# The first batch's v in whole loads: four small loads taken out of a load order

## The chip, the cores and the metric

One core of a Trainium2 chip runs the whole program. The metric is the device time of one execution in microseconds (us). Other engines than TensorE, which does the matrix products (PE in the profile), are VectorE (DVE), ScalarE (ACT), GpSimd (POOL) and SyncE (SP). Loads from memory are issued by an engine's instruction stream and carried out by sixteen DMA engines.

## The reference, cut to what matters

```python
# q, k, v: (8 batches, 8 heads, 576 positions, 64)
scores = scale * np.matmul(q, k.transpose(0, 1, 3, 2))
mask = np.abs(pos[:, None] - pos[None, :]) <= 32
scores = np.where(mask, scores, -1000000000.0)
attn = softmax(scores)
attn_out = np.matmul(attn, v)
x = attn_out.transpose(0, 2, 1, 3).reshape(4608, 512)
h = x @ w_in                     # 512 x 2048
g = np.where(h >= 1, h, np.where(h <= -1, 0.0, (h + 1) ** 2 / 4))
out = g @ w_out                  # 2048 x 512
```

Attention in a sliding window of 32 positions to either side, then a two-layer network with a smoothed ReLU between the layers. The inputs are float32 in memory; the kernel computes in bfloat16, and the loads that GpSimd issues convert on the way.

## The kernel before, in words

**Tiling.** The token axis of the second part (4608) is cut into 18 tiles of 256 tokens (TB). For each tile, eight steps `a` (NF = 8) project 256 of the 2048 hidden columns each: line 489, eight matmuls of 128x256, two pieces of w_in to a step. From step 72 to 135 the steps are wide (line 514). ScalarE and VectorE turn the projected sums `hp` into `gT` (lines 533 to 540). The second product, with w_out, follows eight steps behind; up to step 39 partly in half-width pairs (line 464, `pair`), later in units (line 449). One variable `a` counts all steps, 160 in all, and the list `ev` holds what else is done after a step.

**Attention.** The softmax part of the eight batches is cut into pieces, put between these steps by a hand-written table (`at`, `sl`). `scores` multiplies k and q, `sums` multiplies the exponentials with v and with ones, and `xT` takes the quotients. v lies in `vn` as 18 chunks of 64 positions a pair of heads: chunks 0 to 8 for one head row, 9 to 17 for the other. `sums` over the first 256 positions read chunks 0 to 4 and 9 to 13; the remaining chunks are first read in steps 3 to 5.

**The start.** The first batch comes in halves: `load_half` brings positions 0 to 287 of q and k, then 288 to 575. While they are under way TensorE multiplies zeros (`keep_warm`). Then come the transposes, scores, sums and quotients of the first 256 positions, and step 0 begins. The second halves of q and k are transposed after step 1 (`tposes`, 189), the second batch's q after step 10 and its k after step 12 (lines 415 and 416).

**Loads.** All loads but the first half of q go through GpSimd's queue, in the order of the program text. Before the change this order is:

- k of batch 0, first half, two loads (L86)
- v of batch 0, chunks 0 to 13, four loads (L107, called in lines 132 and 136)
- w_in's first four pieces (L111); a piece is 256 columns for 64 partitions, 128 KB on the chip
- q and k, second half, four loads (L86)
- four times: a piece of w_in, then chunks 14 to 17 of one of v's four parts (lines 149 and 150)
- six more pieces of w_in, the first quarter of half of w_out (L116), w_in's last two, three more of w_out
- q and k of batch 1 (L93), v of batch 1 in four whole loads (L107), the other half of w_out, then batch 2

Batches 3 to 7 are loaded at set steps later.

**Waits.** The framework puts the semaphores in. A matmul waits for the loads that write the region that it reads; a load on GpSimd's queue can also wait, for an older load to land.

Of the kernel before, what the change touches and what calls it, by code (L numbers as in the profile page):

```python
# [14 lines left out]
def kernel(  # L15
# [19 lines left out]
    nc = tc.nc  # L35
# [3 lines left out]
    NC = S // 64  # L39
# [38 lines left out]
    qn, kn, vn = {}, {}, {}  # L78
# [20 lines left out]
            nc.gpsimd.dma_start(out=x[:, :, h], in_=src[b, NY * h:NY * h + NY].rearrange("y s d -> (y s) d")  # L99
                                .rearrange("(u p) d -> p u d", p=128))  # L100

    def load_v(b, n, c0=0, c1=2 * NC):
        if b not in vn:
            vn[b] = nat.tile([128, 2 * NC, 2, D], BF, name="vn", tag="vn", bufs=3)
        h, a = divmod(n, 2)
        y = NY * h + 2 * a
        nc.gpsimd.dma_start(out=vn[b][64 * a:64 * a + 64, c0:c1, h], in_=v[b, y:y + 2].rearrange("y s d -> (y s) d")  # L107
                            .rearrange("(c r) d -> r c d", r=64)[:, c0:c1])

    def load_w_in(c0, c1, h):  # L110
        nc.gpsimd.dma_start(out=w_in[64 * h:64 * h + 64, :, c0:c1],  # L111
# [11 lines left out]
    for h in range(2):  # L123
# [5 lines left out]

    step = early.tile([128, 257], BF, name="step")  # L130
    V.memset(step, 0.0)
    load_v(0, 0, 0, 14)
    P.affine_select(out=step, in_=step, compare_op=ALU.is_ge, fill=-1.0, base=-65, channel_multiplier=-1,
                    pattern=[[1, 257]])
    for n in range(1, 4):
        load_v(0, n, 0, 14)
    V.memset(ones, 1.0)
    for t in qTs:
        V.memset(t[:, 0:PAD], 0.0)
# [4 lines left out]
    def put(todo):  # L144
        for fn, *x in todo:
            fn(*x)

    w = [(load_w_in, c, c + 256, h) for c in range(0, DFF, 256) for h in range(2)]
    put(w[:4] + [(load_half, 1, t, h) for t in range(2) for h in range(2)]
        + [x for n in range(4) for x in (w[4 + n], (load_v, 0, n, 14, 2 * NC))] + w[8:14])  # L150
    put([(load_w_out, 0, 0, 4)] + w[14:])
    put([(load_w_out, 0, k, k + 4) for k in range(4, 16, 4)] + [(load_rows, 1, t) for t in range(2)])
    put([(load_v, 1, n) for n in range(4)])
# [264 lines left out]
    for b in range(LONG + 1, B):  # L418
        a = sl[5 * (b - 1) - 7] - 17
# [75 lines left out]
    for a in range(NF * NB + 2 * NF):  # L495
# [11 lines left out]
        if a < NF * NB:  # L507
            if wide:
                n, f = divmod(a - WIDE[0], 2 * NF)
                t = WIDE[0] // NF + 2 * n  # L510
# [6 lines left out]
            else:  # L517
                t, f = divmod(a, NF)
# [30 lines left out]
        if a >= 40:  # L549
            n = (4, 3, 3)[a % 3] if a < 88 else 4  # L550
# [36 lines left out]
```

## Time and profile before

| | us |
|---|---|
| median of 3 runs | 310.57 (310.31 to 310.81) |
| the profiled execution | 310.31 |
| its span in the profile | 308.5 |
| PE busy | 293.6 (95% of the span) |
| VectorE busy | 240.0 (78%) |
| ScalarE busy | 191.6 (62%) |
| GpSimd busy | 80.4 (26%) |
| mean granted clock of TensorE | 0.998 |

The profile is of one execution. Its span runs from the first to the last instruction; the device time is somewhat longer. "Busy" of PE counts matmuls whose ends are modelled, so 95% doesn't mean PE at its peak. GpSimd's figure counts the time that it takes to issue loads. A wait is given with what ended it; in the chain of waits each row has its start, its length and what it was.

### The profile page before, as it was taken

The page shows a single profiled execution, that of the slowest core. Times are in us where ns is not written, and L with a number is a line of the kernel's source. Part 1 is how long each engine was busy: PE and PEld are TensorE (multiplying, and loading weights), DVE is VectorE, ACT ScalarE, POOL GpSimd, SP SyncE. Part 2 cuts the span into 40 slices and gives each one's busy share as a digit, 9 for nine tenths or more (in the row PEclk, how much of TensorE's full clock was granted, in tenths as well). Part 3 has the DMA queues.
Part 4 walks back from the last instruction along what each step waited for, and adds up shares of the span by engine and source line. Part 5 has one row for each costly group of instructions (what it writes and reads, how often), then busy time and mean ns, then how long its engine had stood idle before and what let it go on. Part 6 is the DMA issues. An engine that isn't in the chain of part 4 may idle for free.

```text
span 308.5 us, 7943 instructions
## 1 busy us (share of the span) xinstructions
PE 293.6 (95%) x3350; PEld 181.4 (59%) x3388; DVE 240.0 (78%) x376; ACT 191.6 (62%) x320; POOL 80.4 (26%) x98
## 2 busy tenths in 40 slices
PE   8877999999999999999999999999999999999995
PEld 4555878876666666666654544444445444446644
DVE  3277468888988989998999998888888888878700
ACT  3786786838766758686766666765666654444311
POOL 8897762009106405402800910000000000000000
PEclk9999999999999999999999999999999999999999
DMA  9999999999999999998999993550001000000121
GB/s 150 188 142 184 197 189 162 170 181 101 150 182 119 172 202 111 169 151 130 144 124 187 121 165 51 113 114 34 36 34 37 34 36 35 36 34 34 54 84 68
DMA packets 137779, 35.67 MB, mean 116 GB/s; under 512 B 122256, under 2 KB 133520, under 8 KB 137744
## 3 DMA queue, kind: packets, MB, share of 16 engines
q0 software_dynamic: 103584, 18.06, 81.1%
q1 hardware_dynamic: 34016, 16.81, 25.5%
q8 instruction: 26, 0.43, 0.6%
q10 hardware_dynamic: 144, 0.29, 0.4%
q14 instruction: 9, 0.07, 0.1%
HBM read 36.70 MB, written 9.44 MB: 150 GB/s over the span
## 4 chain that ended last, share of the span: by engine, by line
PE 85%; DMA 7%; POOL 4%; issue 2%; ACT 1%; POOLq 0%; ACTq 0%
PE op L449 34%; PE hp L489 20%; PE hp L514 18%; PE bb L295 6%; PE op L464 4%; DMA qn<-in_q_dram 3%; PE bb L229 2%; POOL w_in L111 2%; DMA w_in<-in_moe_w_in_dram 2%; DMA qh<-in_q_dram 2%; POOL vn L107 1%; PE op L440 1%; PE tp L189 1%; ACT pt L237 1%; POOL kh L86 0%
## 5 line engine op out<-in xcount | busy, mean ns | idle before, releaser
L533 ACT ACTIVATE rr<-hp 128x512 f32<-128x512 f32 x144 | 85.6, 595 | 88.1 <-PE hp L489 43.7
L449 PE MATMUL op<-w_out,gT 128*128 128x512 bf16 x460 | 119.5, 379 | 5.0 <-issue 4.8
L539 DVE TENSOR_TENSOR mx<-hp,rr 128x512 f32<-128x512 f32 x137 | 94.4, 689 | 25.6 <-ACT rr L533 23.7
L540 DVE SCALAR_TENSOR_TENSOR gT<-rr,mx 128x512 bf16<-128x512 f32 x137 | 94.8, 692 | 4.7
L489 PE MATMUL hp<-xT,w_in 128*128 128x256 bf16 x640 | 83.1, 273 | 3.3 <-DMA w_in<-in_moe_w_in_dram 2.9
L489 PEld LDWEIGHTS <-w_in 128*128 128x128 bf16 x640 | 61.8, 98 | 23.9 <-DMA w_in<-in_moe_w_in_dram 2.8
L449 PEld LDWEIGHTS <-gT 128*128 128x128 bf16 x496 | 46.1, 98 | 45.2
L514 PE MATMUL hp<-xT,w_in 128*128 128x512 bf16 x256 | 65.7, 379 | 0.0
L514 PEld LDWEIGHTS <-w_in 128*128 128x128 bf16 x256 | 25.1, 98 | 30.2
L99 POOL DMA_DIRECT2D qn<-in_q_dram x12 | 14.6, 1221 | 89.7 <-DMA kT<-kn 67.3
L237 ACT ACTIVATE pt<-bb 128x1024 bf16<-128x1024 f32 (+1 forms) x33 | 32.7, 1002 | 4.7 <-PE bb L229 3.1
L107 POOL DMA_DIRECT2D vn<-in_v_dram x36 | 29.7, 851 | 5.0 <-DMA w_out<-in_moe_w_out_dram 4.2
L307 DVE TENSOR_TENSOR xT<-bb,rc 128x512 bf16<-128x512 f32 (+1 forms) x32 | 21.0, 657 | 9.3 <-ACT rc L302 8.4
L453 ACT COPY osb<-op 128x512 f32<-128x512 f32 x31 | 18.0, 580 | 11.4 <-PE op L449 11.1
L302 ACT ACTIVATE rc<-lr 128x512 f32<-128x512 f32 (+2 forms) x40 | 23.5, 587 | 1.3
L301 ACT ACTIVATE lr<-bb 128x512 f32<-128x512 f32 (+2 forms) x40 | 22.0, 551 | 0.1
L203 DVE TENSOR_TENSOR pt<-pt,mask 128x1024 bf16<-128x1024 bf16 (+1 forms) x33 | 20.3, 614 | 0.5 <-ACT pt L237 0.5
L295 PE MATMUL bb<-pt,ones 64*64 64x256 bf16 (+3 forms) x352 | 19.6, 255 | 0.3
L295 PE MATMUL bb<-pt,vn 64*64 64x128 bf16 (+3 forms) x712 | 18.2, 204 | 0.0
L464 PE MATMUL op<-w_out,gT 128*128 128x256 bf16 x128 | 16.5, 273 | 1.0 <-DMA w_out<-in_moe_w_out_dram 1.0
L295 PEld LDWEIGHTS <-ones 64*64 64x64 bf16 x352 | 10.3, 105 | 11.9 <-issue 11.9
L295 PEld LDWEIGHTS <-vn 64*64 64x64 bf16 x712 | 16.7, 107 | 0.0
(61 smaller groups left out, 141.6 us busy)
## 6 DMA issues: line engine op xcount, KB each, us to landing
out_dram<-osb SPq DMA_DIRECT2D x35, 256.0 KB, 2.3
vn<-in_v_dram POOLq DMA_DIRECT2D x28, 144.0 KB, 11.1
qn<-in_q_dram POOLq DMA_DIRECT2D x12, 288.0 KB, 6.3
kn<-in_k_dram POOLq DMA_DIRECT2D x12, 288.0 KB, 8.5
w_in<-in_moe_w_in_dram POOLq DMA_DIRECT2D x16, 128.0 KB, 4.9
w_out<-in_moe_w_out_dram POOLq DMA_DIRECT2D x4, 256.0 KB, 7.9
w_out<-in_moe_w_out_dram POOLq DMA_DIRECT2D x2, 512.0 KB, 14.3
kh<-in_k_dram POOLq DMA_DIRECT2D x4, 144.0 KB, 5.2
```

Of the source, the lines that this page charges most:

```text
L107: nc.gpsimd.dma_start(out=vn[b][64 * a:64 * a + 64, c0:c1, h], in_=v[b, y:y + 2].rearrange("y s d -> (y s) d") .rearrange("(c r) d -> r c ...
L237: A.activation(p, ps[:, :, :w * n].rearrange(like, y=m), AF.Exp, scale=D ** -0.5)
L295: nc.tensor.matmul(bb[HD[h], a, o + c0:o + c1], ones[HD[a]] if c is None else vn[b][HD[a], c, h], p(a, h), start=n == 0, stop=True, skip_g ...
L301: A.activation(lr[:, :, :D0], bb[:, :, D0:2 * D0], AF.Ln)
L302: A.activation(rc[:, :, :D0], lr[:, :, :D0], AF.Exp, scale=-1.0)
L449: nc.tensor.matmul(op[tt], gT[:, j, home(tt // 2), 128 * (tt % 2):128 * (tt % 2) + 128], w_out[:, j], start=j == 0, stop=j == 15)
L464: nc.tensor.matmul(o[:, tt], gT[:, j, p, 128 * tt:128 * tt + 128], w_out[:, j, 256 * half:256 * half + 256], start=not done, stop=len(done ...
L489: nc.tensor.matmul(hp[:, j], w_in[:, kk, 256 * f + 128 * j:256 * f + 128 * j + 128], xT[:, kk, r0:r0 + TB], start=first and n == 0, stop=l ...
L514: nc.tensor.matmul(hp.rearrange("p n t -> p (n t)"), w_in[:, kk, 128 * f:128 * f + 128], xT[:, kk, r0:r0 + 2 * TB], start=n == 0, stop=n == 3)
L533: A.activation(rr, hp, AF.Relu, scale=0.5, bias=0.5)
L539: V.tensor_max(mx, hp, rr)
L540: V.scalar_tensor_tensor(g, rr, 1.0, mx, op0=ALU.min, op1=ALU.mult)
```

## The change

The four small loads of batch 0's chunks 14 to 17 go, and the four early loads bring all 18 chunks. `load_v` loses its range of chunks.

```diff
-    def load_v(b, n, c0=0, c1=2 * NC):
+    def load_v(b, n):
...
-        nc.gpsimd.dma_start(out=vn[b][64 * a:64 * a + 64, c0:c1, h], in_=v[b, y:y + 2].rearrange("y s d -> (y s) d")
-                            .rearrange("(c r) d -> r c d", r=64)[:, c0:c1])
+        nc.gpsimd.dma_start(out=vn[b][64 * a:64 * a + 64, :, h], in_=v[b, y:y + 2].rearrange("y s d -> (y s) d")
+                            .rearrange("(c r) d -> r c d", r=64))
...
-    load_v(0, 0, 0, 14)
+    load_v(0, 0)
...
-        load_v(0, n, 0, 14)
+        load_v(0, n)
...
-    put(w[:4] + [(load_half, 1, t, h) for t in range(2) for h in range(2)]
-        + [x for n in range(4) for x in (w[4 + n], (load_v, 0, n, 14, 2 * NC))] + w[8:14])
+    put(w[:4] + [(load_half, 1, t, h) for t in range(2) for h in range(2)] + w[4:14])
```

Its name: "Second batch's q transposed in slot 10 instead of 11; w_in in pieces of 256 columns throughout, in place of: Second q transposed in slot 10; w_in in 256-column pieces; last 4 of 18 chunks of the first".

## The prediction

> **What bounds the kernel now.** I read the chain of waits first, then the sums of TensorE's (PE's) waits, then the table by two-microsecond windows. The end is PE's: the page gives PE 85% of the chain that ended last and DMA 7%. So I ask where PE still waits for something else, and PE's sums of waits answer: for pieces of w_in and w_out, 3.9 us, plus 4.8 us of "issue", spread in 30 gaps of at most 0.2 us that nothing here touches.
>
> ```profile
> PE op L449 <- issue: 4.8, 30, 0.2
> PE hp L489 <- DMA w_in<-in_moe_w_in_dram: 2.9, 4, 0.9
> PE op L464 <- DMA w_out<-in_moe_w_out_dram: 1.0, 2, 0.7
> ```
>
> In order of time these waits are at 17.62 (0.92 us), 22.42 (0.89), 26.07 (0.69), 27.35 (0.25), 28.79 (0.41) and 30.55 (0.73). After 36.07, where the second batch's q is transposed, PE has no wait for a load left. What the loads cost is therefore settled by the time at which PE gets past 36.07, and the chain shows who set that (start, duration, what):
>
> ```profile
> 6.12 2.38 POOL w_in L111 x4
> 8.49 5.62 DMA qh<-in_q_dram
> 14.12 0.28 issue
> 14.40 0.61 POOL w_in L111
> 15.01 0.61 POOL vn L107
> 15.62 0.61 POOL w_in L111
> ...
> 16.25 0.62 POOL vn L107
> ...
> 16.90 2.41 POOL w_in L111 x4
> 19.32 5.94 DMA w_in<-in_moe_w_in_dram
> 25.25 0.28 issue
> 25.54 10.49 DMA qn<-in_q_dram
> ...
> 36.07 1.20 PE tp L189 x36
> ```
>
> The reader is to see three things. First, GpSimd (POOL) issues loads, and what ends its pauses is the landing of an older load, 0.28 us earlier. Counting its loads in order, the 19th (14.40) waits for the 11th, the 35th (25.54) for the 27th, and the 43rd (36.31, q of batch 2) for the 35th. I conclude that eight loads may be under way and each new one waits for the eighth before it. Second, from 14.40 to 19.32 POOL issues without a pause: the chain is POOL's time. Third, two of the small v pieces, at 15.01 and 16.25, stand in that chain.
>
> The windows (start and end, length, then busy time and count of PE, PE weight loads, DVE, ACT, POOL, clock, DMA, GB/s) show what that costs the transfers:
>
> ```profile
> 18.00:20.00 2.00, 2.00 (x44) 1.37 (x42) 1.59 (x3) 1.22 (x3) 2.00 (x5) 1.00 1.25 120
> 20.00:22.00 2.00, 1.53 (x54) 1.06 (x51) 1.27 (x3) 2.00 (x5) 1.95 (x3) 1.00 1.27 154
> 22.00:24.00 2.00, 1.58 (x37) 1.26 (x38) 1.42 (x3) 1.85 (x4) 1.66 (x3) 1.00 1.03 129
> 26.00:28.00 2.00, 1.68 (x14) 1.39 (x15) 1.97 (x5) 1.24 (x3) 1.43 (x3) 1.00 1.47 202
> ```
>
> From 26 to 36 the five windows move 202, 190, 199, 210 and 206 GB/s, mean 201. The five from 16 to 26 move 154, 120, 154, 129 and 172, mean 146. A pair of a 128 KB w piece and a 32 KB v piece takes POOL 1.23 us, which supplies 164 KB (in thousands of bytes) / 1.23 = 133 GB/s. The dip looks like short supply.
>
> **What goes.** Four load_v calls of 4 chunks leave POOL, from 11.52, 12.96, 15.00 and 16.25. Each cost 0.61 to 0.66 us of POOL, one of the eight places for 3.4 to 5.3 us, and 32 KB of transfer.
>
> **What is added.** The same 32 KB joins each of the first four v loads. Two prices.
> POOL: batch 1's whole v loads take 1.71 us for two, 0.855 each; today's first takes 0.83 and the next three 2.29, 0.763 each. So 0.02 + 3 x 0.092 = 0.30 us, and w_in's first piece goes out at 6.42, not 6.12.
> Transfer: these are rows of 128 bytes on the chip, and the stretch from 6 to 8 us, almost all v, moved
>
> ```profile
> DMA packets 2375, 0.31 MB, mean 154 GB/s; under 512 B 2367, under 2 KB 2375, under 8 KB 2375
> ```
>
> so a piece costs 32.8 KB / 154 = 0.21 us, four 0.85 us. All that is issued behind v lands later by 0.30 (if only POOL counted) to 0.85 (if the DMA engines are never idle there). The engines' slices all read 9 from 6 to 14 us, so I take 0.7.
>
> **Who is hit early.** v's fourth load lands at 10.0 (5.30 plus 4.7) and would land near 10.7; its first use is 10.55, so the first softmax chain is late by 0.15 to 0.35 us. w_in's first four pieces land by 12.65, then 13.35; the projection that needs the last of them is at 13.5 or later. The second half's k lands at 15.95, then 16.65, used at 15.91: its copies have 0.6 us of slack behind VectorE's queue (L537 at 17.02). The first PE wait that grows is 17.62, for w_in's sixth piece. It is 0.7 later less the 0.21 of the one small v piece ahead of it: 0.5 us. PE is then 0.5 late.
>
> **What is won.** In the new order the loads 15 to 24 are w_in pieces without a gap, and the 19th is now w_in's ninth. It waits for the 11th (q, 14.12 + 0.7) plus 0.28: issued at 15.10 against 16.90 today. Three more follow at 0.60 each (2.41 / 4), none held by its eighth predecessor (k's last lands at 16.65, plus 0.28 = 16.93, and that load is due at 16.9). The thirteenth piece waits for the fifth, 16.60 + 0.7 + 0.28 = 17.6, against 19.32. That is 1.7 us earlier. Its landing took 5.94 us. Seven 128 KB pieces are then ahead or in flight where today one 32 KB, one w_in and four more stand, some 0.2 MB more; against that the queue no longer runs dry. I add 0.2. So it lands at 23.75 against 25.25, and q of batch 1, released by it and then 10.49 us under way, lands 1.5 us earlier, at 34.5.
>
> Bounds for this step: at most the whole dip is filled, (201 - 146) GB/s x 10 us = 550 KB, at 201 GB/s 2.7 us. At least 0, if the engines are slow in that stretch for a reason of their own, because the bytes ahead of q are the same in both orders. Of these, 1.5 is nearest to the chain's own rows.
>
> **Can PE use it?** From 17.62 to 36.07 PE waited 0.89 + 0.69 + 0.25 + 0.41 + 0.73 = 2.97 us after the first wait, so 0.5 late at the start leaves 2.5 to gain: enough. ScalarE is nearly full from 18.71 to 26.67 and starts 0.5 late; it makes up about 0.25 in its gaps there and had 0.47 us idle ahead of 27.14. No PE step up to 36.07 hangs on it longer than that. Behind 36.07, k lands at 39.3 (26.27 plus 13.0) for a use at 39.99, v of batch 1 at 44.1 for 45.2, w_out's second half at 46.8 for 48.1. These stand behind the same queue, so they move with q, and their slack of 0.7 to 1.3 us stays. The later loads are placed by PE's own steps. Sum: 310.31 (profiled execution, span 308.5 and 1.8 around it) - 1.5 = 308.8; the median before is 0.26 above that execution, so **309.1**.
>
> **A rule that speaks against it.** In 18 to 24 us VectorE is busy 1.27 to 1.59 us of 2 while the transfers sag. The Trainium skill (SBUF — State Buffer, section on the two separate sides) says that GpSimd cannot write descriptors for its loads while some VectorE operations hold the port that they share. By that the sag follows VectorE's work, stays after the change, and the sum is 310.6 with nothing won. The trace speaks only half for it: from 26 to 28 VectorE is busy 1.97 us and 202 GB/s are moved, though from a longer queue.
>
> **Rivals.** *The sag is not POOL's supply.* For it: from 20 to 24, with no small piece left to issue, POOL issues 128 KB per 0.61 us (215 GB/s) and yet only 154 and 129 are moved. Against it: w_in's first four pieces, issued alike, went at 168 to 195. Then q lands when it does now, the first 0.5 us is paid at 17.62 and taken back at 26.07 and 28.79: 310.5, between 310.2 and 310.9.
> *The v loads cost far more than 0.21 each.* Batch 1's four whole loads, issued at 27.59, 28.44, 29.77 and 30.81, land 13.0 to 13.3 us later, 1.0 to 1.3 us apart; today's four 14-chunk loads land between 8.2 and 10.0, 0.6 apart. At 1.0 apart all behind v is 1.6 late and the w_in chain still wins 0.9. To decide for slower, the delay at 14.12 must pass the 2.5 us between 14.40 and 16.90, by which w_in's ninth piece goes out sooner. At 1.3 apart, 4 x 0.7 = 2.8, and with POOL's 0.30 ahead of it 3.1, that piece is issued 0.6 later than now, q lands 0.6 later: 311.2. Against it: batch 1's loads shared the engines with w_out, and the stretch from 6 to 8 us shows such rows at 154 GB/s.
> *The name tells of more than the edit does.* Second q in slot 10 (L416) and 256-column pieces (L148) stand in the kernel already; only v's split goes. That adds no time of its own.
>
> **Chances.** Forecast 0.58, no supply effect 0.26, v far dearer 0.16. Alone, the forecast's range is 308.2 to 310.0. For 8 in 10 it must take in the second case and part of the third: **308.1 to 311.0**. 0.2% of 310.57, 0.62 us, is about what a measurement can tell from no change. Faster by more: 0.57; within: 0.27; slower: 0.16.
>
> **What would show it.** Right: the chain from 14 us on has w_in issues only, w_in's ninth at about 15.1; the windows from 18 to 24 move over 170 GB/s; PE's waits for w_in sum to under 2 us though the first grows to about 1.4; q of batch 1 is transposed near 34.6. Wrong: w_in's thirteenth piece lands at 25 again, or the first wait exceeds 3 us, or a new wait appears at k, v or w_out of the second batch.

## The result, and the profile after

| | before | changed |
|---|---|---|
| median of 6 runs each, us | 310.66 (310.31 to 311.26) | 308.20 (307.61 to 309.32) |
| ratio | | 0.9926, 95% interval 0.9904 to 0.9948 |
| profiled execution, us | 310.31 | 309.32 |
| its span, us | 308.5 | 307.6 |

The change is worth 2.46 us, by the interval 1.6 to 3.0. The profiled execution of the changed kernel is the longest of its six and that of the kernel before the shortest, so the profiles show only 1.0 us of that. Lines of the changed kernel stand one lower than before (L488 is the projection, L463 the pair).

PE's waits for w_in and w_out (us in all, times, longest) fell from 3.9 to 2.3 us. A wait of 0.3 us at 7.37, for the first half of k, is new:

```profile
PE hp L488 <- DMA w_in<-in_moe_w_in_dram: 2.1, 3, 1.1
PE op L463 <- DMA w_out<-in_moe_w_out_dram: 0.2, 1, 0.2
PE tp L188 <- DMA kh<-in_k_dram: 0.3, 1, 0.3
```

The chain of waits (start, duration, what) up to the transposition of the second batch's q:

```profile
6.64 1.80 POOL w_in L111 x3
8.44 6.91 DMA w_in<-in_moe_w_in_dram
15.34 0.28 issue
15.63 3.01 POOL w_in L111 x5
18.64 6.54 DMA w_in<-in_moe_w_in_dram
25.18 0.28 issue
25.46 9.56 DMA qn<-in_q_dram
...
35.07 1.20 PE tp L188 x36
```

The v issues are gone from the chain, and 36.07 has become 35.07. But a new link stands in front: w_in's fourth piece, issued at 8.44, landed 6.91 us later, where before the four took 4.5 to 4.8. GpSimd (POOL) needed its place among the eight and issued w_in's eighth piece only at 15.63.

The windows (length, busy time and count of PE, PE weight loads, VectorE, ScalarE, POOL; clock, DMA, GB/s last) show the sag filled: 171, 169 and 185 GB/s where 120, 154 and 129 stood.

```profile
18.00:20.00 2.00, 1.34 (x23) 0.99 (x18) 2.00 (x4) 1.58 (x3) 1.91 (x5) 1.00 1.40 171
20.00:22.00 2.00, 1.98 (x46) 1.28 (x44) 1.60 (x3) 1.64 (x3) 2.00 (x4) 1.00 1.36 169
22.00:24.00 2.00, 2.00 (x61) 1.56 (x64) 1.23 (x3) 2.00 (x5) 2.00 (x3) 1.00 1.35 185
```

### The profile page after: what moved, and what is told of

Read it like the earlier page. It is cut to its first block, busy times and chain, and to the rows that moved or that the text cites. A ratio compares the mean times of both kernels' runs of the same rounds, so it can differ in the third digit from the quotient of the medians.

```text
span 307.6 us, 7939 instructions
## 1 busy us (share of the span) xinstructions
PE 292.6 (95%) x3350; PEld 180.9 (59%) x3388; DVE 239.9 (78%) x376; ACT 191.3 (62%) x320; POOL 78.4 (25%) x94
## 4 chain that ended last, share of the span: by engine, by line
PE 85%; DMA 7%; POOL 3%; issue 2%; ACT 1%; POOLq 0%; ACTq 0%
PE op L448 34%; PE hp L488 20%; PE hp L513 18%; PE bb L294 6%; DMA w_in<-in_moe_w_in_dram 4%; PE op L463 4%; DMA qn<-in_q_dram 3%; PE bb L228 2%; POOL w_in L111 2%; POOL vn L107 1%; PE op L439 1%; PE tp L188 1%; ACT pt L236 1%; POOL kh L86 0%; PE bb L253 0%
## 5 line engine op out<-in xcount | busy, mean ns | idle before, releaser
L488 PE MATMUL hp<-xT,w_in 128*128 128x256 bf16 x640 | 83.1, 273 | 2.6 <-DMA w_in<-in_moe_w_in_dram 2.1
L488 PEld LDWEIGHTS <-w_in 128*128 128x128 bf16 x640 | 61.7, 98 | 23.0 <-issue 3.1
L107 POOL DMA_DIRECT2D vn<-in_v_dram x32 | 27.8, 901 | 4.3 <-DMA w_out<-in_moe_w_out_dram 3.8
L463 PE MATMUL op<-w_out,gT 128*128 128x256 bf16 x128 | 16.5, 273 | 0.2 <-DMA w_out<-in_moe_w_out_dram 0.2
```

The costliest lines, as they stand in the source:

```text
L107: nc.gpsimd.dma_start(out=vn[b][64 * a:64 * a + 64, :, h], in_=v[b, y:y + 2].rearrange("y s d -> (y s) d") .rearrange("(c r) d -> r c d", ...
L463: nc.tensor.matmul(o[:, tt], gT[:, j, p, 128 * tt:128 * tt + 128], w_out[:, j, 256 * half:256 * half + 256], start=not done, stop=len(done ...
L488: nc.tensor.matmul(hp[:, j], w_in[:, kk, 256 * f + 128 * j:256 * f + 128 * j + 128], xT[:, kk, r0:r0 + TB], start=first and n == 0, stop=l ...
```

## The experiments

Every kernel ran beside the kernel before on the same chip, and ratios are to that. A small load is one of the four of 32 KB. All 13 profiles taken after the prediction, and the one before, agree in one thing: from the start of the q transposition to the end of the execution it is 274.2 to 274.3 us (310.31 - 36.07, 309.32 - 35.07, and so on). So in the profiles the time differs only by what a kernel does up to that point, and the point is given with each.

| kernel | median, us | ratio (95% interval) | q transposed in its profile |
|---|---|---|---|
| changed, again | 308.11 | 0.9926 (0.9911 to 0.9942) | 34.59 |
| + POOL's time | 308.86 | 0.9941 (0.9922 to 0.9960) | 33.49 |
| + tiny loads | 311.10 | 1.0024 (1.0014 to 1.0035) | 36.48 |
| + five holds | 311.93 | 1.0046 (1.0029 to 1.0063) | 38.20 |
| + one hold | 311.00 | 1.0022 (1.0007 to 1.0037) | 36.56 |
| before, no late v | 307.52 | 0.9903 (0.9885 to 0.9921) | 33.32 |
| before, late v in a block | 309.85 | 0.9982 (0.9967 to 0.9996) | 35.87 |
| before, 512-column pieces | 311.47 | 1.0020 (0.9999 to 1.0042) | 37.54 |
| changed, 512-column pieces | 307.98 | 0.9919 (0.9896 to 0.9943) | 33.41 |
| block and 512-column pieces | 308.48 | 0.9940 (0.9920 to 0.9960) | 36.11 |
| changed, last two of 512 | 308.51 | 0.9932 (0.9917 to 0.9946) | 35.15 |

### What of a small load costs: POOL's time, its place, or its packets

A small load takes POOL some 0.62 us, one of eight places, and 32 KB of transfer. Three kernels bring one or two of these, or the waits alone, back into the changed kernel. The first, POOL's time alone:

```diff
+    idle = const.tile([128, 512], FP, name="idle")
+    def spend():
+        P.memset(idle, 0.0)
...
-    put(w[:4] + [...] + w[4:14])
+    put(w[:4] + [...] + [x for n in range(4) for x in (w[4 + n], (spend,))] + w[8:14])
```

> The changed kernel, with four fillings of a spare tile on POOL (about 0.6 us each) at the points where the four small v loads were: POOL's time comes back, but no place among the eight, no packets. If POOL's time is what was won: about 1.7 us of the gain goes, 309.9 to 310.5. If it was the places or the transfers: as the changed kernel, 308.2 within 0.5.

The second, POOL's time and the place, with 8 KB each:

```diff
+    def load_spare(n):
+        h, a = divmod(n, 2)
+        nc.gpsimd.dma_start(out=spare[64 * a:64 * a + 64, 0, h], in_=v[0, NY * h + 2 * a, 0:64])
...
+    put(w[:4] + [...] + [x for n in range(4) for x in (w[4 + n], (load_spare, n))] + w[8:14])
```

> The changed kernel, with four loads of 64 rows each (8 KB instead of 32) into a spare tile where the four small v loads were: POOL's time and the four places come back, the packets hardly. If places count besides POOL's time: 310.3 to 311, clearly above the kernel with the fillings. If POOL's time alone counts: the same as that kernel, 309.9 to 310.5. If only the transfers count: 308.2.

The third has no small load at all, only the waits that the small loads had brought: a short copy on POOL reads a tile that an older load fills.

```diff
+    def hold(h, of):
+        P.tensor_copy(held[HD[h], 0:64], of()[HD[h], 0, 0:64])
...
+    put(w[:4] + [...] + w[4:6]
+        + [(hold, 0, lambda: qn[0, 1])] + w[6:7] + [(hold, 0, lambda: kn[0, 1])] + w[7:8]
+        + [(hold, 0, piece[2])] + w[8:10] + [(hold, 1, piece[2])] + w[10:12] + [(hold, 0, piece[3])] + w[12:14])
```

> The changed kernel without any small load, but GpSimd made to wait at five points, each time until an older load has landed, as the small loads made it wait in the kernel before: ahead of w_in's 7th piece for q's first load of the second half, ahead of the 8th for k's, ahead of the 9th, 11th and 13th for the 5th, 6th and 7th piece. Theory (a small load costs the place that it takes, because that makes the next large load wait for an older one): the dip to 110 to 150 GB/s between 18 and 24 us comes back, and 309.8 to 311. Rival (the small loads slow the DMA engines by themselves): 308.2 to 308.7, no dip.

The windows of the kernel with the fillings of a tile, then of the one with tiny loads, then of the one with holds:

```profile
18.00:20.00 2.00, 1.57 (x40) 1.29 (x40) 1.17 (x2) 1.22 (x2) 2.00 (x4) 1.00 1.45 193
20.00:22.00 2.00, 2.00 (x72) 1.56 (x60) 1.38 (x2) 2.00 (x6) 2.00 (x4) 1.00 1.34 181
22.00:24.00 2.00, 2.00 (x56) 1.56 (x44) 1.38 (x2) 1.97 (x5) 2.00 (x4) 1.00 1.41 185
```

```profile
18.00:20.00 2.00, 1.68 (x40) 1.27 (x40) 1.11 (x2) 0.95 (x3) 2.00 (x4) 1.00 1.06 109
20.00:22.00 2.00, 2.00 (x68) 1.52 (x56) 1.41 (x3) 2.00 (x6) 2.00 (x4) 1.00 1.17 140
22.00:24.00 2.00, 0.93 (x16) 0.71 (x8) 1.42 (x3) 1.87 (x3) 1.83 (x4) 1.00 0.91 110
```

```profile
18.00:20.00 2.00, 1.43 (x29) 1.11 (x32) 1.66 (x3) 1.16 (x3) 1.74 (x5) 1.00 0.71 83
20.00:22.00 2.00, 2.00 (x70) 1.56 (x62) 1.38 (x2) 2.00 (x5) 1.96 (x4) 1.00 1.15 139
22.00:24.00 2.00, 0.53 (x27) 0.40 (x16) 1.38 (x2) 1.97 (x4) 2.00 (x4) 1.00 1.15 141
```

The first has POOL busy all the time (2.00 of 2.00 in each window) and no sag. Its four fillings, 0.55 us each, cost 0.75 us of the median, with an interval that overlaps the changed kernel's. That lies between the two expectations, nearer to nothing than to the 1.7 us that POOL's time was to cost. The second moves a quarter of the bytes and has the whole sag and the whole loss; at 311.10 it is just above its range and slower than the kernel before, whose early v loads are shorter. The third has neither the loads nor their packets, and has sag and loss, more than was expected (its holds are a little later than the waits before: w_in's ninth piece goes out at 18.34 against 16.90).

What the place does can be seen on POOL. These are w_in's ninth piece and those behind it with the fillings, then w_in's seventh piece and its ninth with those behind it in the kernel with tiny loads:

```profile
15.75 3.70 POOL L111 DMA_DIRECT2D w_in<-in_moe_w_in_dram  x6
```

```profile
15.02 0.63 POOL L111 DMA_DIRECT2D w_in<-in_moe_w_in_dram  x1 [0.99 <-DMA qh<-in_q_dram]
17.75 3.69 POOL L111 DMA_DIRECT2D w_in<-in_moe_w_in_dram  x6
```

Both kernels spend nearly the same time on POOL between the large loads (0.55 and 0.52 us a piece). With tiny loads the ninth piece goes out 2.0 us later, behind waits for older loads to land, and the median is 2.2 us longer. Counted from each load's issue to its landing, 0.42 MB are under way at 18 us with tiny loads, 0.39 with five holds and 0.46 in the kernel before, against 0.79 with the fillings and 0.79 to 0.92 in the profiles of the changed kernel. So the cost of a small load is the place: it makes the next large load wait for an older one to land. The packets cost nothing that shows. POOL's time is nearly free here, but not as a rule: in its three profiles the changed kernel's POOL waits 1.6 to 1.7 us ahead of w_in's eighth piece, a wait that the profile with the fillings does not have, so the fillings may have taken time that was idle otherwise.

### What the longer early loads cost

```diff
-        + [x for n in range(4) for x in (w[4 + n], (load_v, 0, n, 14, 2 * NC))] + w[8:14])
+        + w[4:14])
+    V.memset(vn[0][:, 14:2 * NC], 0.0)
```

> The kernel before without its four small v loads: chunks 14 to 17 of the first batch's v are zeros, written by VectorE, so four chunks of v are left out of the output. POOL and places as in the changed kernel, but the early v loads stay at 14 chunks. Theory: the four longer loads cost 0.5 us at PE's first wait for w_in, paid back later, so between 307.3 and 308.2. Rival (longer early loads cost nothing): 308.2. Rival (they cost 0.85 in full): 307.3.

307.52 against 308.11 for the changed kernel on the same chip: 0.6 us, between the theory and the rival with 307.3. The two ratios' intervals overlap, so the size is not settled.

### A queue that runs dry once

```diff
+    put(w[:4] + [...] + w[4:8] + [(hold, 0, piece[2])] + w[8:14])
```

> The changed kernel with one such wait, ahead of w_in's 9th piece for the 5th to land, so that the queue runs dry once, for about 1.2 us near 20 us. If a dry queue costs only the time that it is dry: 309.0 to 309.6, and full rate again 2 us later. If the engines stay slow after it, as the 110 GB/s at 22 to 24 us in the kernel with 512-column pieces suggests, with loads enough issued: under 160 GB/s in two or three windows behind it, and 309.8 or more.

The hold in POOL's timeline, and the windows behind it:

```profile
17.66 0.23 POOL L152 COPY held<-w_in 64x64 bf16<-64x64 bf16 x1 [2.36 <-DMA w_in<-in_moe_w_in_dram]
17.90 3.67 POOL L111 DMA_DIRECT2D w_in<-in_moe_w_in_dram  x6
```

```profile
18.00:20.00 2.00, 1.59 (x40) 1.28 (x40) 1.49 (x3) 1.16 (x2) 2.00 (x4) 1.00 0.61 68
20.00:22.00 2.00, 2.00 (x70) 1.54 (x60) 1.38 (x2) 2.00 (x6) 2.00 (x4) 1.00 1.24 152
22.00:24.00 2.00, 1.08 (x22) 0.71 (x8) 1.38 (x2) 1.94 (x4) 2.00 (x4) 1.00 0.93 107
24.00:26.00 2.00, 1.70 (x45) 1.31 (x48) 1.85 (x3) 1.74 (x4) 1.80 (x3) 1.00 1.34 165
```

One pause of POOL costs the whole gain and more: 311.00 against 308.1, as the second of the two expectations had it. The reader is to see that the sag does not end with the pause. From 17.90 POOL issues without a gap, 128 KB per 0.61 us, which is 215 GB/s, and still the windows from 20 to 26 move 152, 107 and 165. Against 190 GB/s the three lack 38, 83 and 25, over 2 us each 0.29 MB, and the first window alone 0.24 MB. More is lost behind the dry stretch than in it. It is not a lack of loads under way: at 22 us there are 0.79 MB, as many as in the changed kernel at 18, where 171 GB/s are moved. Why the transfers stay slow, no run here shows.

### Other arrangements

Late v in one block behind w_in's tenth piece:

```diff
+        + w[4:10] + [(load_v, 0, n, 14, 2 * NC) for n in range(4)] + w[10:14])
```

> The kernel before with its four small v loads in one block behind w_in's tenth piece instead of one after each of the fifth to eighth. Theory of places: four of eight places hold 32 KB again, only two to three us later, so the dip moves to about 19 to 23 us and most of the loss stays: 309.5 to 310.5. If it was that the small loads stood among the pieces that PE waits for first, it falls to 307.6 to 308.2.

309.85: most of the loss stays, as for places. The sag moves (149, 137, 147 and 114 GB/s from 18 to 26 us).

Larger pieces of w_in behind the small loads, and the same in the changed kernel:

```diff
-    w = [(load_w_in, c, c + 256, h) for c in range(0, DFF, 256) for h in range(2)]
+    w = [(load_w_in, c, c + 256, h) for c in range(0, 1024, 256) for h in range(2)]
+    w += [(load_w_in, c, c + 512, h) for c in (1024, 1536) for h in range(2)]
```

> The kernel before, its four small v loads where they were, but w_in's last 1024 columns in four pieces of 512 columns (256 KB) instead of eight of 256, and the first quarter of w_out behind them. If what costs is that four of eight places hold 32 KB, then larger pieces in the other places fill the queue again: from 20 us on over 180 GB/s, and 308.6 to 309.6. If the small loads cost by themselves (POOL's time, their packets), the time stays at 310.4 within 0.5. Larger pieces are also complete later, which may take back up to 0.7.

> The changed kernel with w_in's last 1024 columns in pieces of 512 columns. In it all places hold 128 KB or more and the transfers run at 170 to 190 GB/s, so by the theory of places there is little left to win: 308.2 within 0.6. If POOL's time were the bound, four issues fewer (2.4 us) would show: 307 or less.

The first missed: 311.47 instead of 309, no faster than the kernel before. Of the large pieces the first went out at 17.10, with 0.46 MB under way at 17 us; 108 GB/s were moved from 18 to 20. Behind that the transfers were slow (110 from 22 to 24) with all of w_in and the first half of w_out issued by 22.6 and 1.8 MB under way at 22 us. So a queue that is filled again does not bring the rate back at once, which the theory of places had taken for granted. PE then waited for the first 512-column pieces in one go:

```profile
PE hp L490 <- DMA w_in<-in_moe_w_in_dram: 3.5, 1, 3.5
```

In the changed kernel the same pieces give the steadiest windows of all, and a time that can't be told from the changed kernel's:

```profile
18.00:20.00 2.00, 1.54 (x36) 1.20 (x40) 1.41 (x3) 1.02 (x2) 2.00 (x3) 1.00 1.29 203
20.00:22.00 2.00, 2.00 (x73) 1.56 (x63) 1.38 (x2) 2.00 (x6) 1.66 (x3) 1.00 1.22 202
22.00:24.00 2.00, 1.80 (x54) 1.33 (x46) 1.38 (x2) 1.97 (x5) 0.74 (x1) 1.00 1.28 202
```

Both together, late v in a block behind the first two large pieces:

```diff
+        + w[4:10] + [(load_v, 0, n, 14, 2 * NC) for n in range(4)] + w[10:])
```

> Both: early v loads of 14 chunks, w_in's last 1024 columns in pieces of 512 columns, and the four small v loads in one block behind the first two of those. Theory of places: at no time do the eight places hold less than about 0.9 MB, so no dip, and the early part is shorter by the four chunks: 307.4 to 308.2, as the kernel without late v chunks (307.5). Rival (four issues and four places cost wherever they stand): 309.5 to 310.5.

308.48, above the range, with 142 and 134 GB/s at 18 to 20 and 22 to 24 in its profile: "no dip" was wrong, though that profiled execution, 310.35, is the longest of its eleven. And with only the last 512 columns in large pieces:

> The changed kernel with w_in's last 512 columns alone in two pieces of 512 columns: the pieces that steps 4 and 5 wait for stay small, and two loads fewer share the eight places. Theory (the queue is nearly always full in the changed kernel, PE waits little behind 19 us): 307.5 to 308.1, no more than 0.6 below the changed kernel. Rival (loads on GpSimd's queue cost their number): 306.9 or less.

308.51, also above its range. None of these is clearly faster than the changed kernel.

### The changed kernel again, twice

> The changed kernel once more, for a second profile. My theory (POOL's issues and the eight places set the pace of w_in): 308.2 within 0.7, q of batch 1 transposed 2 to 3 us earlier than before (33.5 to 34 us), and no pause of 1.7 us on POOL ahead of w_in's fifth piece from the end of w_in's fourth, which in the first profile landed 6.9 us after its issue. Rival (chance of one execution): the profile shows 35 us again and the gain lies elsewhere.

> The changed kernel, one more profile. In two profiles w_in's fourth piece landed 6.8 to 6.9 us after its issue, and GpSimd waited 1.6 us for its place. If that belongs to the order of the loads, it is there a third time; if it is a matter of where a 16 KB instruction fetch falls, it may be absent, and then the execution takes under 308 us and q of batch 1 is transposed before 34.2.

The time held: 308.11. The other two guesses for the second profile did not: q is transposed at 34.59 instead of 33.5 to 34, and w_in's fourth piece is late in all three profiles, 6.91, 6.83 and 6.82 us after its issue. The chain of the third:

```profile
8.14 6.82 DMA w_in<-in_moe_w_in_dram
14.96 0.28 issue
15.24 2.44 POOL w_in L111 x4
```

The third execution took 310.14 us, q transposed at 35.90. Single executions of this kernel so far lie between 307.6 and 310.1. By the expectation for the third profile, a late piece in all three belongs to the order of the loads. The record does not bear that out: the kernel with the fillings issues the same loads in the same order up to w_in's fifth piece, and there the fourth landed 5.2 us after its issue, in the one with tiny loads 5.1. Nor does the instruction fetch decide: one starts between 12.0 and 13.3 us in every profile, with the late piece and without.

The late piece goes with long executions. In the block with 512-column pieces (6.76 us) and with the last two of 512 (6.67) it is late too, and in these two and the first two profiles of the changed kernel the profiled execution is the longest of its kernel's 5 to 11 runs. The kernels with the fillings and with 512-column pieces, whose fourth piece took 5.2 and 5.5 us, had q at 33.49 and 33.41: 2.6 us won, and the profiled execution with the fillings is the shortest of its six. With one hold it took 6.2 us in one of the shorter executions, but there POOL stands at the hold behind it in any case. So the distance between the changed kernel's profiles (1.0, 1.5 and 0.2 us won) and the medians (2.3 to 2.5) would follow if the piece is late in some executions only. What the executions without a profile do at that point can't be seen, so this is not shown.

## Why the prediction was right, and where it was not

**That the start decides.** Right: 274.2 to 274.3 us follow the start of q's transposition in every profile.

**What is won, 1.5 us to q.** The direction and the mechanism of waiting for the eighth load before were right. The size was 2.46 in the medians, near the 2.7 that the whole sag had been worked out to be worth, and 0.2 to 1.5 in the profiles; 308.20 stands at the very low end of the forecast's own range. The step's own figures did not hold in the profile: w_in's ninth piece, due at 15.10, came at about 16.2, behind a late fourth piece that nothing in the working had, and q's first load of the second half, put at 0.7 us later, landed 1.4 us later (15.56 against 14.12). The thirteenth, due to land at 23.75, landed at 25.18. q came earlier all the same, at 35.03, since its own landing took 9.56 us and not 10.49, which fits with loads ahead of it that were further along. The prediction had named a thirteenth piece at 25 as a sign that it was wrong. The sign came in the profile and the time fell even so, so the path through the thirteenth piece is not what carried the gain there: q, issued at 25.46 against 25.54, landed sooner. That 1.5 lies between what the profile (1.0) and the medians (2.46) show is in part luck.

**"The chain is POOL's time."** This reading failed. The chain showed two v issues at 0.61 us, and the text priced 133 GB/s of supply from POOL's time. With that time put back and the places left free, the sag did not return. The places, named in the same paragraph, carry the loss: 308.86 with POOL's time alone, 311.10 and 311.93 with the places or their waits. Even in that chain the place was there to see: w_in's ninth piece went out at 16.90, 0.28 us after the fifth had landed.

**The longer v loads, 0.5 us at the first wait.** The size is near, the path is not the one named. POOL's part, 0.30 in the working, was 0.52, 0.26 and 0.25 us in the three profiles (w_in's first piece at 6.64, 6.38 and 6.37 against 6.12). The wait that was to grow was the one at 17.62, for w_in's sixth piece. In the first profile PE waited earlier, for the fourth:

```profile
15.48 1.47 PE L488 MATMUL hp<-xT,w_in 128*128 128x256 bf16 x12 [1.11 <-DMA w_in<-in_moe_w_in_dram]
```

Leaving the chunks out gave 0.6 us of the whole time, with the doubt told above.

**The rival that the sag is not POOL's supply.** Half right. Its evidence, slow windows from 20 to 24 while POOL issues 215 GB/s, was real: the engines do stay slow with loads issued. In the kernel with one hold such windows follow a dry queue. In the kernel before the queue ran low and not dry (from 18 to 20 the slowest half microsecond moved 107 GB/s, against 11 with one hold). In the changed kernel it did not run low, and the slow windows are gone. That running low starts them fits all of this; why they last is open.

**The rule on VectorE's port.** VectorE is busy 1.41, 1.38 and 1.38 us in the windows of the changed kernel with 512-column pieces, at 203, 202 and 202 GB/s, and 1.49, 1.38 and 1.38 in those of the kernel with one hold, at 68, 152 and 107. The same VectorE work goes with both, so the rule of the Trainium skill (SBUF — State Buffer, section on the two separate sides) does not decide here. The sag left with the change, which that sum did not allow.

**The rival with dearer v loads.** Its case for a slower kernel was wrong: nothing landed 3 us later. But in the changed kernel's profiles what stands behind the v loads came later than the 0.7 that was put: q's first load of the second half came 1.2 to 1.4 us later (0.75 in the profile with the fillings), close to the rival's milder case, in which the change still wins. Its reading of batch 1 was a little off: those four loads landed 1.4, 0.8 and 1.4 us apart.

## What to carry to other kernels

Where loads wait for the eighth load before them, count what the eight places hold in bytes, not only how many loads there are or how long their issue takes: a 32 KB or 8 KB load in the middle of a stream is paid by the large load that its place would have held. Bytes under way are needed, but they are not enough: behind a stretch that ran low or dry, 0.8 to 1.8 MB under way moved only 107 to 110 GB/s here. Test it by putting back one cost at a time, the issuer's time, the place, the packets, before believing a chain of waits that goes through the issuer. And compare medians: a profiled execution can stand a microsecond from them.

## What the runs showed of the hardware that was not expected

A load queue that ran dry once, near 19 us, moved 68 GB/s in that window and then 152, 107 and 165 in the next three, although POOL had been issuing 215 GB/s since 17.90. In the changed kernel, where it never ran dry, the stretch from 18 to 24 moved 171, 169 and 185, and with 512-column pieces 203, 202 and 202. And in three of three profiles of the changed kernel one 128 KB load, the fourth piece of w_in, needed 6.8 to 6.9 us to land, where w_in's first four had needed 4.5 to 4.8 in the kernel before, and 5.2 was enough in the kernel with the fillings.
